# Products of two neighbouring blocks issued together, and six PSUM banks shared by attention and the second product

**Chip, cores, metric.** One core of a Trainium2 chip. The time is the device time of one execution in microseconds (us), the median of several runs. The profiled run gives a span that is about 1.8 us shorter than the time of its run. The experiments ran in three sets, each on another chip (first `after_again`, `single`, `split_paired`, `key19`; then `lead40`, `lead40_whole`, `cast_first`, `from4_whole`; last `before_again`); across sets, times are compared as ratios to the kernel before.

## The reference, cut to what matters

```python
q, k, v, f_logit: (4, 8, 768, 48)            # batch, heads, steps, head size
f = sigmoid(f_logit)
for t in range(768):
    state = f[t] * state + outer(k[t], v[t])   # per batch and head, 48 x 48
    y[t]  = q[t] @ state
x = y as (3072, 384)
h = x @ w_in                                   # 384 -> 2048
out = softplus(h) @ w_out                      # 2048 -> 384
```

The kernel cuts the 3072 rows into 24 blocks of 128. For each block it does attention in blocked form, and then the two products of the feed-forward part.

## The kernel before

All instructions are tasks. A list scheduler written in the kernel places them, in the order of a key and by estimated costs, into one fixed order per engine. TensorE's work for a block, with the names by which the profile knows the tiles:

- `cs` (decay sums), `qkT` (8 transposes), `pp` (key-query products), `uu` (state update), `oo` (outputs), `xTp` (3 transposes);
- `hh`: the first product, 48 matmuls of 128 columns; `ops`: the second product, 16 matmuls of 384 columns.

The products that the change moves:

```python
def a_p(i, b):                       # block i, b = 0: even heads, 1: odd heads
    ps = att_bank("pp")
    lo = 64 * b
    for p in range(NP):              # four head pairs
        nc.tensor.matmul(out=ps[:, p * 128:(p + 1) * 128],
                         lhsT=qkT_t[i][lo:lo + 48, NP + p, :],
                         rhs=qkT_t[i][lo:lo + 48, p, :], start=True, stop=True, ...)
```

Their contraction has 48 rows, at partitions 0 or 64: the even and the odd heads' products read different rows. The text calls this the half-array mode. Nearly everything else from block 4 on reads 112 or 128 rows. VectorE then multiplies each bank by a mask (`ptm<-pp,mask`) and so frees it. PSUM's eight banks are dealt out so:

```python
def att_bank(name, dt=FP32, cols=512):
    return psum.tile([128, cols], dt, name=name, tag="att", bufs=4)   # all attention tiles, in turn
# hh: tag "hh", bufs=2        ops: tag "ops", bufs=2
```

and the products' tasks, where `s = NJ * i - LEAD` and `LEAD = 40`:

```python
for b in range(2):
    task(("p", i, b), "PE", 0.21, [("ev", i), ("p", i, b - 1)], s + 17 + b / 10,
         a_p, (i, b), "att", [("m", i, b)])
```

`LEAD` says by how many steps of the first product the attention of a block runs ahead. `L770` in the profile is filler: matmuls without use, in the first 24 us, meant to keep TensorE's clock up.

Of the kernel before, what the change touches and what calls it, by code (L numbers as in the profile page):

```python
# [8 lines left out]
FP32 = mybir.dt.float32  # L9
# [5 lines left out]

LEAD = 40
LAG = 24
# [7 lines left out]
BIAS = 164  # L25
LATE = 8
LOADS = 3
SEM = 0.2


class Task:


    def __init__(self, name, engine, cost, needs, key, emit, slot=None):
        self.name, self.engine, self.cost, self.needs, self.key = name, engine, cost, needs, key
        self.emit, self.slot = emit, slot
        self.frees = []
        self.end = None


def in_order(tasks, slots):



    clock = {t.engine: 0.0 for t in tasks if t.engine}
    taken = {n: [[] for _ in range(k)] for n, k in slots.items()}
    count = {n: 0 for n in slots}
    queue = {e: sorted((t for t in tasks if t.engine == e), key=lambda t: t.key) for e in clock}
    behind = {t: [] for t in tasks}
    for t in tasks:  # L50
        for d in t.needs:
            if not t.engine:
                behind[d].append(t)

    def delays(t):
        for d in behind[t]:
            if d.end is None and all(n.end is not None for n in d.needs):
                d.end = max(n.end for n in d.needs) + d.cost
                delays(d)

    def ready(t):
        need = t.needs
        if t.slot:
            need = need + taken[t.slot][count[t.slot] % slots[t.slot]]
        at = 0.0
        for d in need:
            if d.end is None:
                return None
            at = max(at, d.end + (SEM if d.engine != t.engine else 0.0))
        return at  # L70

    order = []
    left = sum(len(w) for w in queue.values())
    while left:
        best = None
        for e, waiting in queue.items():
            first = None
            for t in waiting[:60]:
                r = ready(t)
                if r is None:  # L80
                    continue
                start = max(r, clock[e])
                if first is None or start < first[0] - 0.03:
                    first = (start, t)
                if start <= clock[e]:
                    break
            if first and (best is None or first[0] < best[0]):
                best = first
        start, t = best
        t.start = start  # L90
        t.end = clock[t.engine] = start + t.cost * (2 if t.engine == "PE" and start < COLD else 1)
        queue[t.engine].remove(t)
        left -= 1
        was = []
        if t.slot:
            was = taken[t.slot][count[t.slot] % slots[t.slot]]
            taken[t.slot][count[t.slot] % slots[t.slot]] = t.frees
            count[t.slot] += 1
        t.waits = t.needs + was
        order.append(t)  # L100
        delays(t)
    return order
# [3 lines left out]
def kernel(  # L106
# [111 lines left out]
    def cast_w(n, w, a, eng):  # L218
        t, d = w_t[n, w]
        m = t.shape[2] // 2  # L220
        copy_on(eng, d[:, :, m * a:m * a + m], t[:, :, m * a:m * a + m])

    def att_bank(name, dt=FP32, cols=512):
        return psum.tile([128, cols], dt, name=name, tag="att", bufs=4)

# [309 lines left out]
    def f2(i, j):  # L535
        if j == 0:
            o_ps[i] = psum.tile([128, 512], FP32, name="ops", tag="ops", bufs=2)
        nc.tensor.matmul(out=o_ps[i][:, 0:DM], lhsT=g_t[i][:, j, :], rhs=w_out_bf[:, j, :],  # L538
                         start=(j == 0), stop=(j == NJ - 1), skip_group_check=True)

    def f2_half(h, j):
        i, m = NB - 1, DM // 2
        if j == 0:
            o_ps[i, h] = psum.tile([128, 512], FP32, name="ops", tag="ops", bufs=2)
        nc.tensor.matmul(out=o_ps[i, h][:, 0:m], lhsT=g_t[i][:, j, :],  # L545
                         rhs=w_out_bf[:, j, h * m:h * m + m],
                         start=(j == 0), stop=(j == NJ - 1), skip_group_check=True)
# [80 lines left out]
    for i in range(0, PAIRED, 2):  # L628
        s = NJ * i - LEAD
        for a in range(2):  # L630
# [3 lines left out]
                 [("cs", i, a)])  # L634
            task(("cs", i, a), "PE", 0.35, [("z2", i, a)], t, a_cs2, (i, a), "att",
                 [("eq", i, a)])
# [9 lines left out]
            for k in (1, 0):  # L646
                task(("tr", i, a, k), "PE", 0.22,
                     [("mk" if k else "mq", i, a), None if k else ("tr", i, a, 1)],
                     t + 10 + (1 - k) / 10, a_tr2, (i, a, k), "att" if k else None,
                     [("ev", i, a)])  # L650
            task(("ev", i, a), "DVE", EV, [("tr", i, a, 0)], t + 10.3, a_ev2, (i, a), "qkT2",
                 [("o", i + 1, a)])
            for b in range(2):
                task(("p", i, a, b), "PE", 0.2, [("ev", i, a)], t + 17 + b / 10, a_p2, (i, a, b),
                     "att" if i else "hh", [("m", i, a, b)])
                task(("m", i, a, b), "DVE", 0.68, [("p", i, a, b), ("m", i, a, b - 1)]
                     + [("m", i, 0, 1) if a else ("o", i - 1)], t + 17.2 + b / 10, a_m2, (i, a, b))
        for n in range(2):
            task(("u", i + n), "PE", 0.45 if n else 0.6,
                 [(m, i, a) for a in range(2) for m in ("vb", "mk", "eq")], s + 12 + n, a_u2,  # L660
                 (i, n), "att", [("tt", i + n)])
            for a in range(2):
                task(("o", i + n, a), "PE", 0.3 if i + n else 0.21,
                     [("m", i, a, 1), ("vb", i, 1), ("sn", i + n - 1) if i + n else None,
                      ("o", i + n, 0) if a else ("o", i + n - 1)], s + 23 + n + a / 20, a_o2,
                     (i, n, a), None if a else "att", [("x", i + n)])
            task(("o", i + n), None, 0.0, [("o", i + n, 1)], 0)

    for i in range(NB):
        c, s = i % NC, NJ * i - LEAD  # L670
        if i >= PAIRED:
            task(("z1", i), "ACT", 0.52, [("f", i)], s - 6, z1, (i,))
            task(("z2", i), "ACT", 0.52, [("z1", i)], s - 5.9, z2, (i,), "zz", [("cs", i)])
            task(("cs", i), "PE", 0.165, [("z2", i)], s, a_cs, (i,), "att", [("eq", i)])
            old = [(m, PAIRED - 2, a) for m in ("mk", "mq") for a in range(2)] + [("u", PAIRED - 2)]
# [9 lines left out]
                 [("o", i), ("u", i)])  # L685
            task(("tr", i), "PE", 0.44, [("mq", i)], s + 10, a_tr, (i,), "att", [("ev", i)])
            task(("ev", i), "DVE", EV, [("tr", i)], s + 10.1, a_ev, (i,), "qkT", [("o", i)])
            for b in range(2):
                task(("p", i, b), "PE", 0.21, [("ev", i), ("p", i, b - 1)], s + 17 + b / 10,
                     a_p, (i, b), "att", [("m", i, b)])  # L690
                task(("m", i, b), "DVE", 0.68, [("p", i, b), ("m", i, b - 1)],
                     s + 17.2 + b / 10, a_m, (i, b), None if b else "ptm", [("o", i)])
            if c < NC - 1:
                task(("ec", i), "DVE", 1.26, [("eq", i)], s + 12, a_ec, (i,), "ect",
                     [("sn", i)])
                task(("u", i), "PE", 0.17, [("vb", i), ("tr", i)], s + 12, a_u, (i,), "att",
                     [("tt", i)])
            task(("o", i), "PE", 0.38 if c else 0.21,
                 [("m", i, 1), ("vb", i), ("sn", i - 1) if c else None], s + 23, a_o, (i,),
                 "att", [("x", i)])  # L700
        s = NJ * (i - i % 2 if i < PAIRED else i) - LEAD
        if c < NC - 1:
# [4 lines left out]
             s + 23.1, a_x, (i,), "xx", [("xt", i)])  # L707
        task(("xt", i), "PE", 0.165, [("x", i)], s + 27, a_xt, (i,), "att", [("xe", i)])
        task(("xe", i), "ACT" if i < 3 else "DVE", {"DVE": 0.36, "ACT": 0.49}, [("xt", i)],
             s + 27.1, a_xe, (i,), "xT", [("f1", i, NJ - 1)])  # L710
        s = NJ * i
        for j in range(NJ):
# [11 lines left out]
            if i == NB - 1:  # L724
                for h in range(2):
                    task(("f2", i, j + h * NJ), "PE", 0.085,
                         [("ln", i, j // 8), ("wo", a), ("f2", i, j + h * NJ - 1)],
                         s + j + h * NJ + LAG, f2_half, (h, j), "ops" if j == 0 else None,
                         [("out", i, h)])
                continue  # L730
            task(("f2", i, j), "PE", 0.165,
                 [("ln", i, j // 8), ("wo", a), ("f2", i, j - 1)], s + j + LAG, f2,
                 (i, j), "ops" if j == 0 else None, [("out", i)])
        if i == NB - 1:
# [15 lines left out]
    for n, (w, j) in enumerate(sums):  # L750
        task(("sum", n), "POOL", 1.08, [("at", "wo", w), ("sum", n - 1), ("xe", 4)], SUMS + 6 * n, add_w, (w, j))
    task(("bias mm",), "PE", 0.65, [("sum", len(sums) - 1)], BIAS, bias_mm, (), "att",
         [("bias out",)])
    task(("bias out",), "DVE", 0.5, [("bias mm",)], BIAS + 0.1, bias_out)

    for t in tasks:
        t.needs = [by[n] for n in t.needs if n in by]
        t.frees.extend(by[n] for n in t.until if n in by)
    slots = dict(att=4, hh=2, ops=2, zz=2, zz2=2, ee=2, ect=2, qkp=4, vb=3, qkT=2, qkT2=3, w32=5, ptm=2, xx=2, xT=6,
                 uexp=3, gg=5, osb=12)  # L760
    idle_ps = psum.tile([128, 512], FP32, name="ops", tag="ops", bufs=2)
    idle_from = WARM_FROM
    for t in in_order(tasks, slots):
        if t.engine == "PE":
# [40 lines left out]
```

## Time and profile before

| | before |
|---|---|
| time, median (lowest to highest) | 192.0 us (191.6 to 192.5) |
| span of the profiled run | 190.2 us |
| TensorE busy | 183.8 us, 97% |
| first `hh`, end of the last matmul's stream | 18.88 us, 187.08 us |
| visits to the half-array mode for `pp` (blocks 4 to 23) | 22 |

How to read it: the end of the last stream is the last matmul's start plus 83 ns, the distance of its kind. Where TensorE has no hole, the time can only fall if its own matmuls, or the stops between them, become fewer. The distance from one matmul's start to the next one's start shows what each costs; busy time doesn't, as the records overlap. The lines are in the prediction.

### The profile page before, as it was taken

The page shows a single profiled execution, that of the slowest core. Times are in us where ns is not written, and L with a number is a line of the kernel's source. Part 1 is how long each engine was busy: PE and PEld are TensorE (multiplying, and loading weights), DVE is VectorE, ACT ScalarE, POOL GpSimd, SP SyncE. Part 2 cuts the span into 40 slices and gives each one's busy share as a digit, 9 for nine tenths or more (in the row PEclk, how much of TensorE's full clock was granted, in tenths as well). Part 3 has the DMA queues.
Part 4 walks back from the last instruction along what each step waited for, and adds up shares of the span by engine and source line. Part 5 has one row for each costly group of instructions (what it writes and reads, how often), then busy time and mean ns, then how long its engine had stood idle before and what let it go on. Part 6 is the DMA issues. An engine that isn't in the chain of part 4 may idle for free.

```text
span 190.2 us, 6300 instructions
## 1 busy us (share of the span) xinstructions
PE 183.8 (97%) x2588; PEld 150.1 (79%) x2588; DVE 125.5 (66%) x272; ACT 148.6 (78%) x247; POOL 106.3 (56%) x150
## 2 busy tenths in 40 slices
PE   6899899999999999999999999999999999999993
PEld 6788788778877888788788788788788788788773
DVE  7699774376788767747777877647867867653021
ACT  5573588899979889989779789789789777766770
POOL 8459755458899899934799644424534533500000
PEclk9999999999999999999999999999999999999999
DMA  5999999999999995574898996866695300110112
GB/s 140 271 267 380 383 374 263 168 186 166 192 174 201 150 203 91 107 147 74 175 180 239 218 218 130 166 128 146 148 165 114 97 25 25 41 45 0 41 47 83
DMA packets 98957, 30.29 MB, mean 159 GB/s; under 512 B 92144, under 2 KB 97392, under 8 KB 98928
## 3 DMA queue, kind: packets, MB, share of 16 engines
q1 hardware_dynamic: 98928, 29.89, 71.8%
q8 instruction: 20, 0.33, 0.8%
q14 instruction: 9, 0.07, 0.1%
HBM read 25.17 MB, written 4.72 MB: 157 GB/s over the span
## 4 chain that ended last, share of the span: by engine, by line
PE 85%; SPq 6%; DMA 6%; DVE 1%; issue 0%
PE hh L518 33%; PE ops L538 33%; DMA w<-in_moe_w_in_dram 6%; SPq L143 5%; PE qkT L333 5%; PE pp L418 4%; PE oo L490 2%; PE xTp L504 2%; PE cs L260 2%; PE oo L485 2%; PE uu L435 1%; PE ops L545 1%; SPq L200 1%; PE oo L405 1%; PE biasps L242 0%
## 5 line engine op out<-in xcount | busy, mean ns | idle before, releaser
L518 PE MATMUL hh<-xT,w_in_bf 128*128 128x128 bf16 x1152 | 115.0, 219 | 0.8 <-DVE w_in_bf L214 0.7
L538 PE MATMUL ops<-w_out_bf,gg 128*128 128x384 bf16 x368 | 110.3, 326 | 0.0
L518 PEld LDWEIGHTS <-w_in_bf 128*128 128x128 bf16 x1152 | 88.6, 98 | 22.2 <-DVE w_in_bf L214 1.2
L526 ACT ACTIVATE uexp<-hh 128x512 f32<-128x512 f32 x96 | 56.8, 595 | 24.7 <-PE hh L518 23.7
L532 ACT ACTIVATE gg<-uexp 128x1024 bf16<-128x1024 f32 x48 | 50.7, 1057 | 1.5
L538 PEld LDWEIGHTS <-gg 128*128 128x128 bf16 x368 | 35.0, 98 | 4.7
L315 POOL TENSOR_TENSOR qkp<-kk,ee 128x384 bf16<-128x384 f32 x20 | 18.3, 916 | 24.1 <-ACT ee L307 11.9
L427 DVE TENSOR_TENSOR ptm<-pp,mask 128x512 bf16<-128x512 f32 x40 | 25.8, 687 | 8.5 <-PE pp L418 8.4
L214 DVE COPY qkT<-qkT 128x1024 bf16<-128x1024 bf16 x24 | 16.6, 691 | 17.7 <-PE qkT L333 15.5
L474 POOL TENSOR_TENSOR sst<-tt,ect 48x192 bf16<-48x192 f32 x32 | 16.3, 511 | 20.2 <-DVE tt L465 14.7
L444 DVE STREAM_TRANSPOSE ect<-ee 32x128 bf16<-32x128 bf16 x64 | 19.5, 305 | 2.9 <-ACT ee L311 1.7
L319 POOL TENSOR_TENSOR qkp<-qq,ee 128x384 bf16<-128x384 f32 x20 | 18.4, 918 | 0.1
L214 DVE CAST xx<-oo 128x384 bf16<-128x384 f32 x21 | 11.7, 556 | 6.0 <-PE oo L490 5.6
L565 DVE TENSOR_TENSOR osb<-ops,bias_bc 128x384 f32<-128x384 f32 x15 | 8.4, 558 | 10.6 <-PE ops L538 10.3
L236 POOL TENSOR_TENSOR wsum<-wsum,w 128x384 f32<-128x384 f32 x14 | 14.0, 1001 | 0.4
L333 PE MATMUL qkT<-ident,qkp 128*128 128x128 bf16 x160 | 12.2, 219 | 0.0
L214 POOL CAST vb<-vv 128x384 bf16<-128x384 f32 x20 | 10.1, 506 | 3.5 <-DMA vv<-in_v_dram 2.8
L465 DVE TENSOR_TENSOR tt<-uu,sst 48x192 f32<-48x192 f32 x32 | 11.3, 354 | 0.8
L770 PE MATMUL ops<-negU,ident 128*128 128x128 bf16 x102 | 9.6, 249 | 1.9 <-POOL ident masks.py:199 1.9
L333 PEld LDWEIGHTS <-qkp 128*128 128x128 bf16 x160 | 10.4, 98 | 1.2
L214 DVE COPY xT<-xTp 128x384 bf16<-128x384 bf16 x21 | 7.4, 352 | 5.2 <-PE xTp L504 5.2
L252 ACT ACTIVATE ff<-ff 128x384 f32<-128x384 f32 x20 | 10.2, 512 | 0.5 <-DMA ff<-in_f_logit_dram 0.5
(82 smaller groups left out, 210.9 us busy)
## 6 DMA issues: line engine op xcount, KB each, us to landing
ff<-in_f_logit_dram SPq DMA_DIRECT2D x20, 192.0 KB, 4.3
kk<-in_k_dram SPq DMA_DIRECT2D x20, 192.0 KB, 3.6
qq<-in_q_dram SPq DMA_DIRECT2D x20, 192.0 KB, 4.1
vv<-in_v_dram SPq DMA_DIRECT2D x20, 192.0 KB, 4.4
out_dram<-osb SPq DMA_DIRECT2D x19, 192.0 KB, 2.1
w<-in_moe_w_in_dram SPq DMA_DIRECT2D x4, 768.0 KB, 9.1
w<-in_moe_w_out_dram SPq DMA_DIRECT2D x4, 768.0 KB, 9.8
f<-in_f_logit_dram SPq DMA_DIRECT2D x4, 192.0 KB, 4.0
```

The lines of the kernel that those rows point to most:

```text
L214: on[eng].tensor_copy(out=out, in_=in_)
L236: nc.gpsimd.tensor_tensor(out=wsum, in0=wsum, in1=t[:, j, :], op=ALU.add)
L315: on[eng].tensor_tensor(out=qkp_bufs[i % 4][:, H:2 * H, 0:D], in0=in_t.pop(("k", i)), in1=e_bufs[i % 2][:, H:2 * H, 0:D], op=ALU.mult)
L319: on[eng].tensor_tensor(out=qkp_bufs[i % 4][:, 0:H, 0:D], in0=in_t.pop(("q", i)), in1=e_bufs[i % 2][:, 0:H, 0:D], op=ALU.mult)
L333: nc.tensor.transpose(ps[:, a * 128:(a + 1) * 128], qkp[:, a, :], ident)
L427: nc.vector.tensor_tensor(out=ptm_t[i].rearrange("p (a b) t -> p b a t", b=2)[:, half, :, :], in0=p_ps.pop((i, half)).rearrange("p (a t) - ...
L444: nc.vector.transpose(out=t[32 * r:32 * r + 32], in_=e[96:128, 0:NP, 32 * r:32 * r + 32])
L474: on[eng].tensor_tensor(out=sn[lo:hi, :, e0:e0 + D], in0=tt[lo:hi], in1=ec[lo:hi].unsqueeze(2).to_broadcast([48, NP, D]), op=ALU.mult)
L518: nc.tensor.matmul(out=h_ps[i, j // 4][:, j % 4, :], lhsT=w_in_bf[:, r, j * 128:(j + 1) * 128], rhs=xT_t[i][:, r, :], start=(r == 0), stop ...
L526: nc.scalar.activation(out=u_t[i, a // 2][:, 4 * (a % 2):4 * (a % 2) + 4, :], in_=h_ps.pop((i, a)), func=AF.Exp, bias=0.0, scale=1.0)
L532: nc.scalar.activation(out=g_t[i][:, 8 * a:8 * a + 8, :], in_=u_t.pop((i, a)), func=AF.Ln, bias=0.5, scale=0.5)
L538: nc.tensor.matmul(out=o_ps[i][:, 0:DM], lhsT=g_t[i][:, j, :], rhs=w_out_bf[:, j, :], start=(j == 0), stop=(j == NJ - 1), skip_group_check ...
```

## The change

Intent: go into the half-array mode once for two blocks instead of once for each. Four banks must then be free at one time, so attention and `ops` share six banks, and each task takes the one that comes free first. The lead grows to 48.

```diff
-LEAD = 40
+LEAD = 48
+BANKS = 6
+SWITCH = 0.09
+PKEY = 17
+GFROM, GTO = 6, 24
+GROUP = 2
...
+        if t.engine == "PE":                                # the scheduler's own estimate
+            if (t.name[0] == "p") != tiled:
+                tiled = not tiled
+                t.end = clock["PE"] = t.end + SWITCH
...
+        if t.slot == "bank":
+            t.bank = free_bank(t)[1]                        # the bank free first
+            was, held[t.bank] = held[t.bank], t.frees
...
-        return psum.tile([128, cols], dt, name=name, tag="att", bufs=4)
+        return psum.tile([128, cols], dt, name=name, tag=f"bank{bank[0]}", bufs=1)
...
-            o_ps[i] = psum.tile([128, 512], FP32, name="ops", tag="ops", bufs=2)
+            o_ps[i] = att_bank("ops")
...
+            size = GROUP if GFROM <= i < GTO else 1
+            g = i - i % size
             for b in range(2):
-                task(("p", i, b), "PE", 0.21, [("ev", i), ("p", i, b - 1)], s + 17 + b / 10,
-                     a_p, (i, b), "att", [("m", i, b)])
+                task(("p", i, b), "PE", 0.125, [("ev", g + size - 1), ("ev", i), ...],
+                     NJ * (g + size - 1) - LEAD + PKEY + (i - g) / 5 + b / 10,
+                     a_p, (i, b), "bank", [("m", i, b)])
```

(The tasks of other kinds get `"bank"` for `"att"` or `"ops"` in the same way; the masks' keys move with the pair's; the filler takes the sixth bank until 24 us.)

More of the change, by code (lines that the diff above doesn't have):

```diff
@@ L37, in __init__, with in_order @@
         self.frees = []
-        self.end = None
-def in_order(tasks, slots):
+        self.end = self.bank = None
+def in_order(tasks, slots, banks):
     clock = {t.engine: 0.0 for t in tasks if t.engine}
@@ L59, in delays, with after @@
                 delays(d)
-    def ready(t):
-        need = t.needs
-        if t.slot:
-            need = need + taken[t.slot][count[t.slot] % slots[t.slot]]
-        at = 0.0
+    held = [[] for _ in banks]
+    def after(need, t, at=0.0):
         for d in need:
@@ L70, in ready, with free_bank @@
         return at
+    def free_bank(t):
+        free = [(after(h, t, at), n) for n, (h, at) in enumerate(zip(held, banks))]
+        return min((f for f in free if f[0] is not None), default=None)
+    def ready(t):
+        need = t.needs
+        if t.slot == "bank":
+            at, free = after(need, t), free_bank(t)
+            return None if at is None or free is None else max(at, free[0])
+        if t.slot:
+            need = need + taken[t.slot][count[t.slot] % slots[t.slot]]
+        return after(need, t)
     order = []
+    tiled = False
     left = sum(len(w) for w in queue.values())
@@ L94, in in_order @@
         was = []
-        if t.slot:
+        if t.slot == "bank":
+            t.bank = free_bank(t)[1]
+            was, held[t.bank] = held[t.bank], t.frees
+        elif t.slot:
             was = taken[t.slot][count[t.slot] % slots[t.slot]]
@@ L221, in cast_w @@
         copy_on(eng, d[:, :, m * a:m * a + m], t[:, :, m * a:m * a + m])
+    bank = [None]
     def att_bank(name, dt=FP32, cols=512):
-        return psum.tile([128, cols], dt, name=name, tag="att", bufs=4)
+        return psum.tile([128, cols], dt, name=name, tag=f"bank{bank[0]}", bufs=1)
     wsum = consts.tile([128, DM], FP32, name="wsum")
@@ L543, in f2_half @@
         if j == 0:
-            o_ps[i, h] = psum.tile([128, 512], FP32, name="ops", tag="ops", bufs=2)
+            o_ps[i, h] = att_bank("ops")
         nc.tensor.matmul(out=o_ps[i, h][:, 0:m], lhsT=g_t[i][:, j, :],
@@ L634 @@
                  [("cs", i, a)])
-            task(("cs", i, a), "PE", 0.35, [("z2", i, a)], t, a_cs2, (i, a), "att",
+            task(("cs", i, a), "PE", 0.35, [("z2", i, a)], t, a_cs2, (i, a), "bank",
                  [("eq", i, a)])
@@ L648 @@
                      [("mk" if k else "mq", i, a), None if k else ("tr", i, a, 1)],
-                     t + 10 + (1 - k) / 10, a_tr2, (i, a, k), "att" if k else None,
+                     t + 10 + (1 - k) / 10, a_tr2, (i, a, k), "bank" if k else None,
                      [("ev", i, a)])
@@ L653 @@
             for b in range(2):
-                task(("p", i, a, b), "PE", 0.2, [("ev", i, a)], t + 17 + b / 10, a_p2, (i, a, b),
-                     "att" if i else "hh", [("m", i, a, b)])
+                task(("p", i, a, b), "PE", 0.11, [("ev", i, a)], t + 17 + b / 10, a_p2, (i, a, b),
+                     "bank" if i else "hh", [("m", i, a, b)])
                 task(("m", i, a, b), "DVE", 0.68, [("p", i, a, b), ("m", i, a, b - 1)]
@@ L660 @@
                  [(m, i, a) for a in range(2) for m in ("vb", "mk", "eq")], s + 12 + n, a_u2,
-                 (i, n), "att", [("tt", i + n)])
+                 (i, n), "bank", [("tt", i + n)])
             for a in range(2):
@@ L665 @@
                       ("o", i + n, 0) if a else ("o", i + n - 1)], s + 23 + n + a / 20, a_o2,
-                     (i, n, a), None if a else "att", [("x", i + n)])
+                     (i, n, a), None if a else "bank", [("x", i + n)])
             task(("o", i + n), None, 0.0, [("o", i + n, 1)], 0)
@@ L673 @@
             task(("z2", i), "ACT", 0.52, [("z1", i)], s - 5.9, z2, (i,), "zz", [("cs", i)])
-            task(("cs", i), "PE", 0.165, [("z2", i)], s, a_cs, (i,), "att", [("eq", i)])
+            task(("cs", i), "PE", 0.165, [("z2", i)], s, a_cs, (i,), "bank", [("eq", i)])
             old = [(m, PAIRED - 2, a) for m in ("mk", "mq") for a in range(2)] + [("u", PAIRED - 2)]
@@ L685 @@
                  [("o", i), ("u", i)])
-            task(("tr", i), "PE", 0.44, [("mq", i)], s + 10, a_tr, (i,), "att", [("ev", i)])
+            task(("tr", i), "PE", 0.44, [("mq", i)], s + 10, a_tr, (i,), "bank", [("ev", i)])
             task(("ev", i), "DVE", EV, [("tr", i)], s + 10.1, a_ev, (i,), "qkT", [("o", i)])
+            size = GROUP if GFROM <= i < GTO else 1
+            g = i - i % size
             for b in range(2):
-                task(("p", i, b), "PE", 0.21, [("ev", i), ("p", i, b - 1)], s + 17 + b / 10,
-                     a_p, (i, b), "att", [("m", i, b)])
+                task(("p", i, b), "PE", 0.125, [("ev", g + size - 1), ("ev", i), ("p", i, b - 1) if b else ("p", i - 1, 1)],
+                     NJ * (g + size - 1) - LEAD + PKEY + (i - g) / 5 + b / 10,
+                     a_p, (i, b), "bank", [("m", i, b)])
                 task(("m", i, b), "DVE", 0.68, [("p", i, b), ("m", i, b - 1)],
-                     s + 17.2 + b / 10, a_m, (i, b), None if b else "ptm", [("o", i)])
+                     NJ * (g + size - 1) - LEAD + PKEY + 0.2 + (i - g) / 5 + b / 10, a_m, (i, b), None if b else "ptm", [("o", i)])
             if c < NC - 1:
@@ L695 @@
                      [("sn", i)])
-                task(("u", i), "PE", 0.17, [("vb", i), ("tr", i)], s + 12, a_u, (i,), "att",
+                task(("u", i), "PE", 0.17, [("vb", i), ("tr", i)], s + 12, a_u, (i,), "bank",
                      [("tt", i)])
@@ L699 @@
                  [("m", i, 1), ("vb", i), ("sn", i - 1) if c else None], s + 23, a_o, (i,),
-                 "att", [("x", i)])
+                 "bank", [("x", i)])
         s = NJ * (i - i % 2 if i < PAIRED else i) - LEAD
@@ L707 @@
              s + 23.1, a_x, (i,), "xx", [("xt", i)])
-        task(("xt", i), "PE", 0.165, [("x", i)], s + 27, a_xt, (i,), "att", [("xe", i)])
+        task(("xt", i), "PE", 0.165, [("x", i)], s + 27, a_xt, (i,), "bank", [("xe", i)])
         task(("xe", i), "ACT" if i < 3 else "DVE", {"DVE": 0.36, "ACT": 0.49}, [("xt", i)],
@@ L727 @@
                          [("ln", i, j // 8), ("wo", a), ("f2", i, j + h * NJ - 1)],
-                         s + j + h * NJ + LAG, f2_half, (h, j), "ops" if j == 0 else None,
+                         s + j + h * NJ + LAG, f2_half, (h, j), "bank" if j == 0 else None,
                          [("out", i, h)])
@@ L732 @@
                  [("ln", i, j // 8), ("wo", a), ("f2", i, j - 1)], s + j + LAG, f2,
-                 (i, j), "ops" if j == 0 else None, [("out", i)])
+                 (i, j), "bank" if j == 0 else None, [("out", i)])
         if i == NB - 1:
@@ L751 @@
         task(("sum", n), "POOL", 1.08, [("at", "wo", w), ("sum", n - 1), ("xe", 4)], SUMS + 6 * n, add_w, (w, j))
-    task(("bias mm",), "PE", 0.65, [("sum", len(sums) - 1)], BIAS, bias_mm, (), "att",
+    task(("bias mm",), "PE", 0.65, [("sum", len(sums) - 1)], BIAS, bias_mm, (), "bank",
          [("bias out",)])
@@ L758 @@
         t.frees.extend(by[n] for n in t.until if n in by)
-    slots = dict(att=4, hh=2, ops=2, zz=2, zz2=2, ee=2, ect=2, qkp=4, vb=3, qkT=2, qkT2=3, w32=5, ptm=2, xx=2, xT=6,
+    slots = dict(hh=2, zz=2, zz2=2, ee=2, ect=2, qkp=4, vb=3, qkT=2, qkT2=3, w32=5, ptm=2, xx=2, xT=6,
                  uexp=3, gg=5, osb=12)
-    idle_ps = psum.tile([128, 512], FP32, name="ops", tag="ops", bufs=2)
+    idle_ps = psum.tile([128, 512], FP32, name="ops", tag=f"bank{BANKS - 1}", bufs=1)
     idle_from = WARM_FROM
-    for t in in_order(tasks, slots):
+    for t in in_order(tasks, slots, [0.0] * (BANKS - 1) + [WARM_TO]):
+        bank[0] = t.bank
         if t.engine == "PE":
```

## The prediction

> **What bounds the kernel now.** I read the page's busy table and forty slices first, then the chain of work that ended last.
>
> ```profile
> PE 183.8 (97%) x2588; PEld 150.1 (79%) x2588; DVE 125.5 (66%) x272; ACT 148.6 (78%) x247; POOL 106.3 (56%) x150
> PE   6899899999999999999999999999999999999993
> PE 85%; SPq 6%; DMA 6%; DVE 1%; issue 0%
> ```
>
> TensorE is busy from slice 7 to slice 39, and 85% of the closing chain is its own work. "Busy" can flatter TensorE, because the records overlap and their ends are modelled, so I looked at the busy time by stretch, and then, in the trace, at the distance from one matmul's start to the next one's.
>
> ```profile
> core 0: us, PE busy (x) PEld busy (x) DVE busy (x) ACT busy (x) POOL busy (x), PEclk, DMA share, GB/s
> ...
> 18.80:30.00 11.20, 10.35 (x178) 8.62 (x176) 8.20 (x16) 7.36 (x11) 7.92 (x11) 1.00 1.06 377
> 30.00:90.00 60.00, 60.00 (x833) 48.46 (x831) 41.03 (x91) 53.87 (x93) 43.96 (x59) 1.00 0.92 159
> 90.00:183.00 93.00, 93.00 (x1289) 75.15 (x1287) 60.13 (x132) 75.25 (x122) 41.60 (x59) 1.00 0.54 120
> ```
>
> From 30 to 183 us TensorE has no hole. By starts: an hh matmul follows another after 56 ns (mean 56.1 of 842), an ops matmul takes 162 to 163 ns, and no distance after 29 us is longer than its kind, with one exception: around the key-query products (tile pp). This is the timeline of TensorE there; columns are start, time from first start to last end, engine, line.
>
> ```profile
> 106.54 0.33 PE L538 MATMUL ops<-w_out_bf,gg 128*128 128x384 bf16 x1
> 106.70 0.33 PE L518 MATMUL hh<-xT,w_in_bf 128*128 128x128 bf16 x3
> 106.96 0.41 PE L418 MATMUL pp<-qkT 48*128 48x128 bf16 x8
> 107.30 0.34 PE L538 MATMUL ops<-w_out_bf,gg 128*128 128x384 bf16 x1
> 107.47 0.33 PE L518 MATMUL hh<-xT,w_in_bf 128*128 128x128 bf16 x3
> ```
>
> The three hh matmuls should take 3 x 56 = 168 ns; pp starts 260 ns after them. Eight pp matmuls have eight 128-column streams, yet the next ops starts 340 ns later. Their starts come in pairs, 14 ns apart in a pair and 56 ns from pair to pair: the first product reads partitions 0 to 47, the second 64 to 111, and the two run beside each other. So eight stream in 4 x 56 = 224 ns. The last hh to the first pp is 152 ns, 96 more than 56; from there to the next ops start 339 ns. Together 152 + 339 - 56 = 435, of which 224 is streaming: **a visit to the half-array mode costs 0.21 us beside its work**. Such a stop is TensorE's own; the wait view shows no engine behind it.
>
> The start is the only other place with slack:
>
> ```profile
> 18.20 0.84 PE L770 MATMUL ops<-negU,ident 128*128 128x128 bf16 x12
> 18.88 0.83 PE L518 MATMUL hh<-xT,w_in_bf 128*128 128x128 bf16 x12
> 19.64 0.51 PE L379 MATMUL uu<-vb,qkp 64*128 64x96 bf16 x8
> ...
> 20.72 1.51 PE L518 MATMUL hh<-xT,w_in_bf 128*128 128x128 bf16 x24
> 22.07 0.27 PE L770 MATMUL ops<-negU,ident 128*128 128x128 bf16 x2
> 22.27 0.41 PE L359 MATMUL pp<-qkT 48*64 48x128 bf16 x8
> 23.43 1.60 PE L518 MATMUL hh<-xT,w_in_bf 128*128 128x128 bf16 x24 [0.75 <-DVE w_in_bf L214]
> 24.96 0.41 PE L359 MATMUL pp<-qkT 48*64 48x128 bf16 x8
> 25.47 0.76 PE L518 MATMUL hh<-xT,w_in_bf 128*128 128x128 bf16 x9
> ```
>
> L770 is filler that keeps the clock up. The first useful hh is at 18.88; w_in arrives in four parts, cast by VectorE at about 18.0, 20.0, 22.7 and 24.7, and hh waits for the third and fourth. From the starts, idle time between 18.88 and 25.5 is 0.75 + 0.17 + 0.82 = 1.74 us.
>
> **What the Trainium skill says.** "TensorEngine Tiling (Array Packing)", Key Properties: changing the tiling mode, not just the tile, drains TensorE. The trace agrees, 96 ns on the way in (18 of 18 hh to pp between 151 and 152 ns). "TensorE: Matmul & The Clock Gate", Part 3, The mechanism: matmuls in different row groups overlap. The trace agrees for different rows (14 ns inside a pair). The same page, "Wait - 56ns, not 53.3ns?": warm 128-column matmuls follow after 55.6 ns; here 56. "PSUM - Partial Sum Buffer", Specifications: 8 banks per partition. Before, they are split 4 (attention), 2 (second product), 2 (hh); after, 6 shared and 2 (hh).
>
> **The change part by part.** No arithmetic changes. I counted in the built order of both programs.
>
> (a) Grouping. Before, the 160 pp matmuls of the later 20 blocks make 22 visits: 18 of eight and 4 of four (two blocks have their halves apart). After, 13: seven of sixteen, two of twelve, two of four, two of eight. Nine fewer x 0.21 = **1.9 us** off TensorE, all of it in the stretch without holes. Streaming time doesn't change: a row group has as many 56 ns steps.
>
> (b) The start. Counting all half-array runs from the first useful hh on, before has 30 and after 18; the other three that go (two uu, one pp of the paired blocks) are now ahead of the first hh, with 13 fewer fillers between. First I test the sum on before: full-array matmuls 153.5 us (each count times its distance: 56 for 128 columns, 163 for 384, 83 for 192, 42 for 96, 26 for 48), half-array streams 6.9, 30 visits x 0.21 = 6.3, idle 1.74, from 18.88: 187.3 us. The trace's last matmul ends its stream at 187.1. After: 153.4 + 6.0 + 18 x 0.21 = 163.2 us. Its first hh comes later: the sixteen pp end at 18.20 as before, then 5 fillers (0.28), the uu piece (19.64 to 20.72 before, so 1.08) and eight pp (0.32): 19.9. Idle after that: the first two w_in parts are used up by 22.9 and the third is usable at 23.43, 0.5; then the first state output needs masks which VectorE takes after its third cast (tt to 24.0, a mask of 0.69), 0.75. The fourth w_in cast now stands behind three masks, at about 25.9 for 24.7, but TensorE meanwhile does all four outputs of blocks 2 and 3 (some 0.47 each), which before lay behind 25.5. So 19.9 + 163.2 + 1.25 = 184.35 against 187.3 by the same sum: **2.9 us**, of which 1.9 is grouping and 1.0 the start.
>
> (c) The tail. The last 8 ops, 32 halves and the two stores stand in the same order in both; 3.1 us after the last matmul stay.
>
> (d) Banks. Nothing is added in work; what may come is waits. A pair of neighbours holds four of six banks at once and VectorE frees them in turn:
>
> ```profile
> L427 DVE TENSOR_TENSOR ptm<-pp,mask x40: 681/686/693, 42.0 to 170.7; 128x512 bf16<-128x512 f32 x40
> ```
>
> In the trace the first mask starts 0.43 us after the first pp, the second 0.61 after it, and both are over 1.72 after the first pp. In the new order about 2.1 us of TensorE work stand between the first pp of blocks 14 and 15 and the output of 14, and some 3.5 before that of 15, whose masks need 0.43 + 3 x 0.61 + 0.69 = 2.95. The margins are 0.4 to 0.5, about what before had at its tightest (0.29). I take 0.1 us for waits here.
>
> Sum: 192.0 - 2.9 + 0.1 = 189.2; I say **189.0**, as the reserve of the start leans towards more.
>
> **The rivals.** (1) Bank waits eat the gain. For: two groups break into 12 and 4, a sign that the order itself found no fourth bank, and ops holds one or two banks for most of a block (7 us). Against: VectorE is busy 60 of 93 us in the long stretch, and its idle rows there wait for TensorE. Nine groups losing 0.3 us each would give 191.7; I hold it for one in ten. (2) The start gives nothing, because the casts, now behind masks, move everything by as much as is saved: 192.0 - 1.9 = 190.1. (3) All holes of the start fill up: 1.9 + 1.74 + 0.4 of filler, no later hh, 188.0, just beyond 2%. (4) A visit of sixteen doesn't stream in pairs (the second block's products wait at the joint until the first's are through): with 0.11 us, two steps, lost in each of nine groups, 1 us comes back, 190.0.
>
> **Range and chances.** The grouping is counted and surest (1.6 to 2.0 us); the start lies between 0 and 2; waits cost 0 to 1. That gives 188.0 to 190.6. The 2% line is at 188.2 and needs rival 3. Faster by over 2%: 0.18; within 2%: 0.79; slower: 0.03.
>
> **What would show it right or wrong.** After, pp should come in seven rows of sixteen lasting about 0.45 us from first to last start, with 96 ns ahead of each; TensorE busy throughout from 30 us to its end; the last matmul near 184; first hh near 19.9; the waits of TensorE for VectorE tiles near zero. It's wrong if TensorE shows waits for masks or for osb after 30 us, if starts inside a sixteen aren't paired, or if the first hh comes after 20.5.

## The result

| | before | after |
|---|---|---|
| time, median | 192.03 us (4 runs) | 189.38 us (4 runs, 188.92 to 189.96) |
| ratio | | 0.9862 (95% interval 0.9824 to 0.9901) |
| span of the profiled run | 190.2 us | 187.9 us |
| first `hh`, end of the last stream | 18.88, 187.08 us | 20.51, 184.76 us |
| `pp` visits of blocks 4 to 23 | 22 | 13 |

A ratio is the mean time of one kernel's fast runs over that of the other's of the same rounds, so it isn't quite the ratio of the medians. The prediction said 189.0 us, 188.0 to 190.6.

The changed kernel's page and its busy time by stretch (columns as in the prediction; line numbers are those of the changed file, where `hh` is L545, `ops` L565, `pp` L445):

```profile
PE 181.0 (96%) x2576; PEld 148.8 (79%) x2576; DVE 123.6 (66%) x272; ACT 146.6 (78%) x247; POOL 106.2 (57%) x150
PE   6699999999999999999999999999999999999993
PE 92%; DMA 3%; ACT 1%; SPq 1%; POOL 0%; issue 0%; DVE 0%; POOLq 0%
```

```profile
20.50:30.00 9.50, 9.13 (x161) 8.10 (x158) 7.68 (x16) 7.33 (x12) 6.81 (x9) 1.00 1.06 380
30.00:184.80 154.80, 154.80 (x2150) 126.45 (x2147) 99.67 (x224) 128.95 (x215) 85.95 (x118) 1.00 0.69 137
```

TensorE is still what bounds it: no hole from 30 us to its end. It simply ends sooner. Here is its timeline around one pair of blocks:

```profile
122.42 0.33 PE L565 MATMUL ops<-w_out_bf,gg 128*128 128x384 bf16 x1
122.58 0.33 PE L545 MATMUL hh<-xT,w_in_bf 128*128 128x128 bf16 x3
122.85 0.64 PE L445 MATMUL pp<-qkT 48*128 48x128 bf16 x16
123.42 0.34 PE L565 MATMUL ops<-w_out_bf,gg 128*128 128x384 bf16 x1
```

Sixteen `pp` take 570 ns from their first start to the next task's start. Before, eight took 340. The way in is the same (`pp` starts some 264 ns after the first of three `hh`, which stream for 168). In ns, exact starts from the traces: a visit of eight costs 435 in all (96 way in, 339 after), of sixteen 664 (95 and 569), of twelve 646, of four 422. Take off the streaming of 56 per pair (224, 448, 448, 224), and each visit costs 198 to 216 beside its streaming, from four `pp` to sixteen.

So all `pp` visits of blocks 4 to 23, summed in the trace, took 9.51 us before and 7.66 after: **1.85 us** of the 2.32 by which the last streams of the two traces end apart (the medians differ by 2.65). The other 0.5 us is gained before 30 us, at the start; after that the changed kernel has 0.2 us of small stops that the kernel before hasn't. These are its lines in the changed kernel; before, they stood as the prediction shows them.

```profile
18.34 0.44 PE L386 MATMUL pp<-qkT 48*64 48x128 bf16 x16
18.71 0.45 PE L801 MATMUL ops<-negU,ident 128*128 128x128 bf16 x5
19.10 0.51 PE L406 MATMUL uu<-vb,qkp 64*128 64x96 bf16 x8
...
20.51 1.51 PE L545 MATMUL hh<-xT,w_in_bf 128*128 128x128 bf16 x24
...
24.85 0.37 PE L432 MATMUL oo<-vb,ptm 64*128 64x48 bf16 x8
25.58 0.83 PE L545 MATMUL hh<-xT,w_in_bf 128*128 128x128 bf16 x12 [0.36 <-ACT uexp L553]
26.24 0.25 PE L426 MATMUL oo<-sst,qkT 112*128 112x96 bf16 x2
```

The `uu` work now stands where filler stood. `hh` starts later, but then runs on with one short idle time in this view, 0.36 us, put down to ScalarE's exponential (it frees the `hh` bank). Before, TensorE idled here for 0.75 us (0.82 by starts) and for 0.17 us more at 25.3 us. The waits of TensorE in the changed kernel, all of them (who waited for whom, us in total, times, longest):

```profile
PE ops L801 <- POOL ident masks.py:199: 1.9, 1, 1.9
PE qkT L370 <- DVE qkp L323: 1.0, 1, 1.0
PE qkT L370 <- POOL qkp L323: 0.7, 1, 0.7
PE hh L545 <- ACT uexp L553: 0.4, 1, 0.4
```

None is for a mask or for the copy that frees an `ops` bank: sharing the banks cost no wait that this view shows.

### The profile page after: what moved, and what is told of

It is laid out like the page before. It is cut to its first block, busy times and chain, and to the rows that moved or that the text cites. A ratio compares the mean times of both kernels' runs of the same rounds, so it can differ in the third digit from the quotient of the medians.

```text
span 187.9 us, 6273 instructions
## 1 busy us (share of the span) xinstructions
PE 181.0 (96%) x2576; PEld 148.8 (79%) x2576; DVE 123.6 (66%) x272; ACT 146.6 (78%) x247; POOL 106.2 (57%) x150
## 4 chain that ended last, share of the span: by engine, by line
PE 92%; DMA 3%; ACT 1%; SPq 1%; POOL 0%; issue 0%; DVE 0%; POOLq 0%
PE hh L545 34%; PE ops L565 32%; PE qkT L360 5%; PE pp L445 3%; DMA q<-in_q_dram 3%; PE xTp L531 2%; PE oo L517 2%; PE cs L287 2%; PE oo L512 2%; PE ops L801 2%; PE uu L462 1%; PE ops L572 1%; PE oo L432 1%; PE qkT L370 1%; PE uu L406 1%; SPq L168 1%
## 5 line engine op out<-in xcount | busy, mean ns | idle before, releaser
L545 PE MATMUL hh<-xT,w_in_bf 128*128 128x128 bf16 x1152 | 109.4, 219 | 0.4 <-ACT uexp L553 0.4
L565 PE MATMUL ops<-w_out_bf,gg 128*128 128x384 bf16 x368 | 104.6, 326 | 0.0
L545 PEld LDWEIGHTS <-w_in_bf 128*128 128x128 bf16 x1152 | 85.7, 98 | 19.4 <-issue 0.6
L553 ACT ACTIVATE uexp<-hh 128x512 f32<-128x512 f32 x96 | 55.5, 594 | 24.5 <-PE hh L545 24.3
L565 PEld LDWEIGHTS <-gg 128*128 128x128 bf16 x368 | 34.8, 98 | 5.7 <-issue 0.2
L454 DVE TENSOR_TENSOR ptm<-pp,mask 128x512 bf16<-128x512 f32 x40 | 25.1, 684 | 5.5 <-PE pp L445 5.4
L334 ACT ACTIVATE ee<-cs 128x384 bf16<-128x384 f32 x20 | 9.5, 476 | 1.4 <-PE ops L565 0.8
L283 ACT ACTIVATE zz<-ff 128x384 bf16<-128x384 f32 x20 | 10.4, 519 | 0.3
```

Of the source, the lines that this page charges most:

```text
L454: nc.vector.tensor_tensor(out=ptm_t[i].rearrange("p (a b) t -> p b a t", b=2)[:, half, :, :], in0=p_ps.pop((i, half)).rearrange("p (a t) - ...
L545: nc.tensor.matmul(out=h_ps[i, j // 4][:, j % 4, :], lhsT=w_in_bf[:, r, j * 128:(j + 1) * 128], rhs=xT_t[i][:, r, :], start=(r == 0), stop ...
L553: nc.scalar.activation(out=u_t[i, a // 2][:, 4 * (a % 2):4 * (a % 2) + 4, :], in_=h_ps.pop((i, a)), func=AF.Exp, bias=0.0, scale=1.0)
L565: nc.tensor.matmul(out=o_ps[i][:, 0:DM], lhsT=g_t[i][:, j, :], rhs=w_out_bf[:, j, :], start=(j == 0), stop=(j == NJ - 1), skip_group_check ...
```

## The experiments

My theory: a visit to the half-array mode costs about 0.21 us of TensorE's time beside its work, and the time follows the count of visits; the start adds up to 1 us. The main rival: the gain comes from the shared banks and the longer lead (fewer waits, an earlier fill), and the pairing is incidental. Further rivals: pairing costs bank waits; the start is set by the loads and gives nothing.

In the table, "by ratio" is (ratio - 1) x 192.1 us; "by visits" is the sum of the `pp` visits of blocks 4 to 23 in the trace, less 9.51 of before; the rest is the difference. The intervals of the ratios are 0.0024 to 0.0045 to either side, some 0.5 to 0.9 us, so a single rest says little and the set says more.

| run | `pp` runs, count x size | visits us | median us | ratio | by ratio | by visits | rest |
|---|---|---|---|---|---|---|---|
| before | 18x8, 4x4 | 9.51 | 192.1 | 1 | | | |
| after_again | 7x16, 2x12, 2x8, 2x4 | 7.66 | 189.67 | 0.9864 | -2.6 | -1.85 | -0.8 |
| single | 19x8, 2x4 | 9.11 | 191.70 | 0.9959 | -0.8 | -0.40 | -0.4 |
| split_paired | 1x16, 5x12, 5x8, 11x4 | 10.73 | 192.90 | 1.0038 | +0.7 | +1.22 | -0.5 |
| key19 | 9x16, 2x8 | 6.84 | 188.50 | 0.9813 | -3.6 | -2.67 | -0.9 |
| lead40 | 3x16, 4x12, 4x8, 8x4 | 9.71 | 192.59 | 1.0023 | +0.4 | +0.20 | +0.2 |
| lead40_whole | 9x16, 2x8 | 6.85 | 189.33 | 0.9857 | -2.7 | -2.66 | -0.1 |
| cast_first | as after | 7.66 | 190.17 | 0.9905 | -1.8 | -1.85 | 0.0 |
| from4_whole | 10x16 | 7.76 (6.64 without a wait) | 190.94 | 0.9945 | -1.1 | -1.75 | +0.7 |

All outputs are right.

The count of visits alone doesn't order these runs: `split_paired` has 22 visits as before, `lead40` has 19. What the time follows is their sum, and it has two parts. Each visit costs about 0.2 us beside its streaming. And four `pp` that have no four of the other half beside them stream for 224 ns, as long as eight. Counting 224 for each eight or lone four, the streaming is 4.93 us before and 4.93 after, 4.48 in `key19`, 5.82 in `lead40` and 6.27 in `split_paired`; what is left of the sums is 4.6, 2.7, 2.4, 3.9 and 4.5 us.

**after_again: the changed kernel once more.** No edit.

> The changed kernel once more, for a second trace and a closer ratio. Counting theory (nine visits to the half-array mode fewer, each 0.21 us, plus a start that depends on when the first loads land): 189.4 us, pp visits of sixteen lasting 664 ns again, first hh anywhere from 19.9 to 20.6 us as the q load lands. Rival (the later first hh of 20.5 us is made by the change itself): first hh at 20.5 again within 0.1 us.

Measured: 189.67 us, ratio 0.9864. The visits are the same to the nanosecond or two. The first `hh` came at 20.65 us, outside the 20.6 that I had given and outside the rival's 20.4 to 20.6 too. Over all traces the sixteen early `pp` start 10.2 us after the first q load has landed, and the load lands where it will: 8.11 and 8.24 us in the two traces of the changed kernel.

**single: the pairing alone undone.**

```diff
-GROUP = 2
+GROUP = 1
```

> Shared banks and longer lead as in the changed kernel, but no pairing of blocks (group size 1). The built order up to the first hh is the same; pp visits are 19 of eight and 2 of four instead of 13. Counting theory: 19 x 435 + 2 x 422 = 9.11 us in pp visits against 7.66, so 1.45 us more than the changed kernel: 190.8 us. Rival (the gain comes from sharing the banks and the lead): within 0.3 us of the changed kernel, 189.4.

Measured: 191.7 us, the mean of its runs 1.8 us over that of after_again in the same rounds. The rival falls: with shared banks and the lead in place but no pairing, most of the gain is gone. The counted 1.45 us is in the trace (9.11 against 7.66 us). In its profiled run, the slowest of six (190.84 to 192.32), the third part of the weights landed at 24.05 us and not at 22.2, and TensorE idled for it (0.7 us in the wait view); the 0.4 us left over are within the scatter.

**split_paired: pairing without the shared six.**

```diff
-            o_ps[i] = att_bank("ops")
+            o_ps[i] = psum.tile([128, 512], FP32, name="ops", tag="ops", bufs=2)
 # and the same for the halves of the last block, the filler and the tasks' slots
-    for t in in_order(tasks, slots, [0.0] * (BANKS - 1) + [WARM_TO]):     # BANKS = 6
+    for t in in_order(tasks, slots, [0.0] * BANKS):                       # BANKS = 4
```

> Pairing and lead as in the changed kernel, but four banks for attention and two for the second product (each attention task still takes the one free first). The built order then has pp runs of 1 x sixteen, 5 x twelve, 5 x eight, 11 x four. Counting theory: 0.66 + 5 x 0.646 + 5 x 0.435 + 11 x 0.424 = 10.7 us in pp visits against 7.66 changed and 9.52 before, so about 3.1 us over the changed kernel: 192.4 us, no gain over before. Rival (pairing pays with any banks): 190.

Measured: 192.9 us, ratio 1.0038 (1.0003 to 1.0072), no gain over before. So the two halves of the change need each other. A pair takes four banks; with four for all of attention, the scheduler puts the later products wherever a bank comes free, and pairs fall into pieces. The timeline of one pair here:

```profile
111.25 0.41 PE L445 MATMUL pp<-qkT 48*128 48x128 bf16 x8
111.58 0.34 PE L565 MATMUL ops<-w_out_bf,gg 128*128 128x384 bf16 x1
111.85 0.40 PE L445 MATMUL pp<-qkT 48*128 48x128 bf16 x4
112.18 0.34 PE L545 MATMUL hh<-xT,w_in_bf 128*128 128x128 bf16 x3
...
112.78 0.40 PE L445 MATMUL pp<-qkT 48*128 48x128 bf16 x4
113.11 0.34 PE L565 MATMUL ops<-w_out_bf,gg 128*128 128x384 bf16 x1
```

Three visits for two blocks. Four `pp` alone take 0.33 us to the next task, as long as eight (0.33 to 0.34), for nothing runs beside them.

**key19: all pairs kept whole.**

```diff
-PKEY = 17
+PKEY = 19
```

> The changed kernel with the products' priority key at 19 instead of 17: all nine pairs stay whole (9 runs of sixteen, 2 of eight). Counting theory: 9 x 664 + 2 x 435 = 6.85 us against 7.66, so 0.8 us less: 188.6 us. Rival (bank waits grow as four banks are taken at once in all groups): TensorE waits for masks or out copies appear in the trace and the time stays at 189.4 or more.

Measured: 188.5 us, ratio 0.9813 (0.9769 to 0.9858), the lowest ratio. The means of the same rounds differ by 1.0 us from after_again, counted 0.8: some 0.4 by two visits fewer and some 0.4 in streaming, as no four run alone. Its page has the same holeless row as the changed kernel's, and the wait view lists no mask and no `ops` copy:

```profile
109.11 0.33 PE L565 MATMUL ops<-w_out_bf,gg 128*128 128x384 bf16 x1
109.37 0.64 PE L445 MATMUL pp<-qkT 48*128 48x128 bf16 x16
109.94 0.34 PE L545 MATMUL hh<-xT,w_in_bf 128*128 128x128 bf16 x3
```

At this pair (blocks 14 and 15) the changed kernel has a visit of twelve and one of four (an `ops` row between them is left out):

```profile
109.05 0.62 PE L445 MATMUL pp<-qkT 48*128 48x128 bf16 x12
...
109.87 0.39 PE L445 MATMUL pp<-qkT 48*128 48x128 bf16 x4
```

So nine pairs at once aren't too many for six banks; that rival falls too.

**lead40: the lead undone.**

```diff
-LEAD = 48
+LEAD = 40
```

> The changed kernel with the lead of attention over the first product back at 40. In the built order the pairs break up: pp runs of 3 x sixteen, 4 x twelve, 4 x eight, 8 x four, and the paired uu stand behind the first hh as before the change. Counting theory: 1.99 + 2.58 + 1.74 + 3.39 = 9.7 us in pp visits, 2.05 more than changed, and the start as before: 192 us. Rival (the lead only moves priorities and the pairing holds the gain): 189.5 to 190.

Measured: 192.59 us. Again the pairs break, the visits are back at 9.71 us, and the gain is gone, though banks are shared and blocks are paired by their keys. In its trace TensorE also idles for 0.7 us at 33 us (for a cast of the second weights) and for 0.4 us at 90.5 us (for a copy of `xT`). These 1.1 us stand after 30 us, so this run's rest of +0.2 says nothing about the start. The lead, the banks and the keys are one setting: what counts is the order that comes out.

**lead40_whole: whole pairs with the start of before.** In the scheduler, on top of `LEAD = 40` (the condition and the list are put in words here):

```diff
+            if FOUR and t is the first product of a pair and at is not None:
+                all_free = sorted(times at which banks come free)
+                if len(all_free) < 2 * GROUP:
+                    return None
+                return max(at, all_free[2 * GROUP - 1])
```

> Lead 40, but a pair's first product is placed only where four banks come free, so that all nine pairs stay whole (9 x sixteen, 2 x eight, as in key19) while the start stands as before the change. It tells the start's share apart: pp visits 6.85 us, 2.67 less than before, so if the start of the changed kernel is worth nothing, this takes what key19 takes, 188.5 us (192.15 - 2.67 = 189.5 by the other way of counting: the start is then worth 1.0). My prediction's step on the start (1.0 us) expects 189.5.

Measured: 189.33 us, ratio 0.9857. Its `pp` visits are those of key19 (6.85 us); the two differ in the lead, and thus in the start and in what follows from it, and in what keeps the pairs whole (this rule, or the key). It takes what the visits alone give (-2.66 of -2.7). Key19 gains 0.85 us more (ratios 0.9813 and 0.9857, in different rounds on another chip, with intervals that overlap). With the rests in the table the same picture: the four kernels of the first set with the new start have -0.8, -0.4, -0.5 and -0.9, mean -0.65; this one, with the old start, -0.1. The traces give less. The end of the last stream less the `pp` visits is 177.57 and 177.22 us in the two traces of before and 177.34 here, but 177.10, 177.03 and 177.00 in after, after_again and key19: 0.33 us earlier in the mean. So the start is worth some 0.3 to 0.6 us, and the two traces of one kernel differ by as much.

**cast_first: the weights' cast ahead of the masks.**

```diff
-SHIFT = {}
+SHIFT = {("cast", "wi", 3, 0): -4}
```

> The changed kernel with VectorE's cast of the fourth part of the first weights ahead of the three masks of blocks 2 and 3, as it stood before the change. Counts of visits are the same. Theory (the outputs of blocks 2 and 3 fill the wait for the weights): with the cast first they come after the weights, TensorE idles for them, up to 1 us is lost, 189.7 to 190.6. Rival (the weights' arrival sets the pace at the start whatever stands around it): no change within 0.3 us, 189.5.

Measured: 190.17 us, ratio 0.9905, about 0.8 us slower than after_again by the ratios, whose intervals overlap; its trace's last stream ends 0.5 to 0.6 us after those of the changed kernel. The start's gain is gone, as far as this can tell. But the reason that I gave isn't quite what the trace shows:

```profile
22.42 2.19 PE L545 MATMUL hh<-xT,w_in_bf 128*128 128x128 bf16 x33
25.36 1.00 PE L545 MATMUL hh<-xT,w_in_bf 128*128 128x128 bf16 x15 [0.74 <-ACT uexp L553]
26.19 0.25 PE L426 MATMUL oo<-sst,qkT 112*128 112x96 bf16 x2
```

The wait is put down to ScalarE's exponential, which frees the `hh` bank, and by place this `hh` still uses the third part of the weights. In the changed kernel an output of block 2 stands between those two rows and covers half of this wait (0.36 us left in the view). So at the start TensorE waits for ScalarE as much as for weights, and the outputs fill the hole because VectorE has done their masks by then.

**from4_whole: one pair more.**

```diff
-GFROM, GTO = 6, 24
+GFROM, GTO = 4, 24
 # and the rule of four free banks as in lead40_whole
```

> All ten pairs from block 4 on grouped and kept whole (10 x sixteen). Counting theory: 0.21 us less than key19, 188.3 us. Rival (block 4's products wait for block 5's loads and masks, and both outputs come late at 45 to 55 us, where TensorE has little else ready): TensorE idles there by more than the 0.21 us saved, 189 to 190.5.

Measured: 190.94 us, ratio 0.9945: slower than key19 by some 2.5 us (by ratios of different sets) for one visit less. It isn't key19 with one pair more: it has the key of the changed kernel and the rule. The timeline there:

```profile
45.64 0.64 PE L451 MATMUL pp<-qkT 48*128 48x128 bf16 x16
47.32 0.66 PE L571 MATMUL ops<-w_out_bf,gg 128*128 128x384 bf16 x3 [1.05 <-ACT gg L565]
```

TensorE waits 1.05 us for ScalarE's logarithm (`gg`) right behind the pair, and 0.65 us more in two waits at 52 us, for `cs` and `hh`. So the rival is right as to the effect: with blocks 4 and 5 held together, TensorE had nothing ready. What the view names is ScalarE, not masks. That other work had been brought forward is my reading and isn't shown. The rest of its loss (its profiled run was faster than its median) isn't traced.

**before_again: the start of the kernel before.** No edit, one look.

> The kernel before once more, for a second trace of its start. If the later start of the changed kernel's TensorE chain (sixteen pp at 18.3 to 18.5 us in four traces, 17.8 in the one of before) is the luck of the loads, the q load of blocks 0 and 1 lands anywhere from 7.7 to 8.5 us here too and the sixteen pp follow 10.1 to 10.3 us after it. If the change makes it, q lands near 7.7 and the sixteen pp start near 17.8 again.

Measured: 191.65 us; q landed at 7.66 us, the sixteen `pp` started at 17.81. In the other traces q landed between 7.67 (lead40_whole) and 8.47 us. Whether two traces at the early end are luck or the kernel before helps the load, stays open; against the latter stand its unchanged order of loads and lead40_whole, which has most of the change and lands as early. Wherever it lands, the chain behind it follows at about 10.2 us, in every kernel.

## Why the prediction was right

**The bound.** Right. TensorE has no hole from 30 us to its end in the changed kernel.

**(a) Grouping, 1.9 us.** Right, in count and size: 22 visits to 13, and 1.85 us in the trace. Single gives most of it back. Key19 takes the next 0.8 us, 0.4 with two visits fewer and 0.4 by streaming no four alone. Lead40 and split_paired lose it: most of their pairs are broken, and with 19 and 22 visits the sums are 9.71 and 10.73 us. That lone fours cost streaming is not in the prediction's rule of 0.21 us per visit; it could leave that out, as the streaming is 4.93 us in both of its kernels. Sixteen stream in pairs throughout (664 - 448 = 216 ns beside the streaming, 211 for eight), so rival 4 (a loss at the joint) falls.

**(b) The start, 1.0 us.** Right in direction, too large: 0.3 to 0.6 us by the runs. The step that failed is the idle time before, 1.74 us = 0.75 + 0.17 + 0.82. It has one wait twice: 0.75 is the view's idle time ahead of the `hh` at 23.43 us, and 0.82 is the same wait by starts. By starts the trace has 0.82, 0.17 and a stop of 0.08. Without the 0.75 the sum for before is 186.6 and not 187.3, and the same subtraction leaves 2.2 us: 1.9 for grouping and 0.3 for the start. That the wrong sum came so near to the trace's 187.08 was luck: it also leaves out 0.4 us, as the two matmuls `biasps` take 0.71 us to the next task and are counted as 2 x 163 ns (in both kernels, so this cancels). Rival 3 rests on the same 1.74.

For the changed kernel two further steps were off and nearly cancelled. The first `hh` came at 20.51 us, for a predicted 19.9: the chain began 0.5 us later because the first q load landed later, which a single trace of before couldn't tell. One of the prediction's own signs of being wrong, a first `hh` after 20.5, thus came true, by a hair. And the idle time after it, before 30 us, was about 0.6 us by starts for 1.25. I expected a wait for the third part of the weights and one for a mask; the trace names ScalarE's exponential. I had looked at the casts of VectorE and not at ScalarE, which must free the `hh` banks.

**(c) The tail.** Right: 3.10 us after the last stream for 3.11.

**(d) Bank waits, 0.1 us.** Right: none in the view, 0.2 us of small stops after 30 us in the starts, none of them named for a mask. Rival 1 didn't come.

The sum in time is -2.65 us for -3.0. The mechanism, fewer visits, carries 1.85 us of it and is shown; the start, counted too large, is hardly more than what two traces of one kernel differ by.

## What to carry to other kernels

On an engine without holes, look for stops that no other engine causes: compare start-to-start distances with those of the same instruction elsewhere. Here a visit to the half-array mode cost 0.2 us beside its streaming, for four products as for sixteen, so fewer, longer visits paid, as long as both halves of the rows had work in them. A batch needs its buffers at one time: pairing without a larger shared pool gained nothing, and it has to be checked in the built order that batches stay whole. And when idle time is added up, take all of it from one measure: the view's gap and the distance of starts show the same wait twice.

## What the Trainium skill lacked or had wrong

- "TensorEngine Tiling (Array Packing)", Key Properties, says that a change of tiling mode drains TensorE, and gives no size. Here: 96 ns on the way in, 198 to 216 ns for a whole visit beside its streaming, for four to sixteen matmuls.
- "TensorE: Matmul & The Clock Gate", Part 3, The mechanism, says that matmuls are in program order "in start AND end". Here the program has four matmuls of the upper rows after four of the lower. In lone visits of four the semaphore increment stands on the fourth; in program order, a visit of eight should have it on the fourth and the eighth. By start time the increments stand on the seventh and eighth, in all 18 visits of eight of the kernel before, and starts come in pairs some 14 ns apart, one pair per 56 ns: by these starts the two row groups run like two queues.
- The same page, Back-to-back issue gap, puts a sustained stream of 128-column matmuls, each with its weight load, at about 81 ns. Here 842 `hh` matmuls with a weight load each follow one another after 56.1 ns in the mean, which is what the page calls the isolated gap.
